# Weight gradients of a gated feed-forward block on one core: the seven block products in another order and other buffers, and the stores of transposed `dd` on another DMA queue

## The chip, the cores and the metric

The kernel runs on one core of one Trainium2 chip. The metric is the device time of one execution in microseconds; the number shown is the median of several runs. The profile is one execution taken by the hardware profiler, and its span runs from the first to the last instruction of the program. TensorE is PE in the profile (its weight loads are PEld), VectorE is DVE, ScalarE is ACT, GpSimd is POOL and SyncE is SP. SP computes nothing here: it only issues DMAs, one after the other, and an instruction of SP or POOL that waits holds up all that stand behind it on that engine.

## The reference

One layer of a transformer, forwards and backwards: layer norm, linear attention with 32 heads, a residual, layer norm again, a gated feed-forward block, a residual; the output and six gradients are returned (for the input and five weight matrices). There are 2048 rows, a width of 640 and a feed-forward width of 1728, all in bf16.

```python
def _B_ref(x, w_gate, w_up, w_down):
    g = _silu(x @ w_gate)
    u = x @ w_up
    return (g * u) @ w_down
...
x = A_x
h = x + _A_ref(_layernorm(x, axis=-1), A_wqkv, A_wo)
h2 = h + _B_ref(_layernorm(h, axis=-1), B_w_gate, B_w_up, B_w_down)
...
_out, _vjp = jax.vjp(_f, A_x, A_wqkv, A_wo, B_w_gate, B_w_up, B_w_down)
_grads = _vjp(grad_out)
```

The change lies in the feed-forward block. With `hn` the normalised rows and `dh2` the incoming gradient, `dg` and `du` are the gradients of `x @ w_gate` and `x @ w_up`, and the weight gradients are `hnᵀ dg`, `hnᵀ du` and, for `w_down`, `mᵀ dh2` with `m = g * u`.

## The kernel before

**Stages.** The program first does the attention forwards, then the second layer norm (to about 150 us of the span), then the feed-forward block forwards and backwards (about 150 to 480 us), then the gradient through both layer norms and the attention, and last the output `h2`. Only the feed-forward stage is changed.

**Groups.** That stage (L616 to L826) runs over four groups of columns of the feed-forward width, `GW = [448, 448, 448, 384]`; the text calls them group 0 to 3 and writes `w` for the width. Each group has two parts.

- *The loop* (L636 to L679) goes over the 16 row tiles of 128 rows, two at a time. PE makes `pg` and `pu` (L640, L645; in group 2 also `pdm`, L655). ACT takes them from PSUM with two sigmoids and two copies (L661 to L667). DVE makes `m`, `dg` and `du` in seven operations (L673). `m` goes to the strip `m_s`, `dg` and `du` side by side to the strips `dd[0]` (row tiles 0 to 7) and `dd[1]` (row tiles 8 to 15). For each row tile SP issues a DMA transpose `stg<-dd` (L676) into one of three staging buffers `stg`, and POOL stores that buffer to `scr_dT` in DRAM (L677), from where the next stage reads it as `cols`. For every four row tiles POOL stores `m_s` to `scr_m` (L679).
- *The dw part* (L703 to L826) makes the weight gradients on PE. `dw` (L703) makes whole products over all 16 row tiles: 16 matmuls for each part it is given. The calls are named here by what they make: `dw(0,1)`, `dw(2,3)` and `dw(4)` for the row blocks of `dh2ᵀ m`, and `dw(dgu 4)` for the last row block of `hnᵀ dg` and `hnᵀ du`. The remaining four row blocks of those two are made as one 2 by 2 block matrix product with seven products of sums in place of eight; each product is done for two row blocks `u` of 128 and has 8 matmuls for each. The sums of `hn` blocks are `S`; the sums of `dd` blocks T1, T2 and T3 are written over `B11` and `B12`, which lie in `dd[0]`, and T4 over the first half of `m_s`.

**Order.** In this stage SP, PE, DVE and ACT run in the order in which the code is written (`manual_schedule`, L616); POOL's order is chosen by the scheduler. After `dw(0,1)` and `dw(dgu 4)` PE does the seven products in the order of L783 to L824: `B11` into `pa` for both `u`, `B21` into `pd` for `u` = 0, `dw(4)`, T1 into `pc`, `B21` for `u` = 1, T1 for `u` = 1, `dw(2,3)`, and then S2 T2, S3 T3, `hn` T4 into `pa` and S4 `B22` into `pc` for the two `u` in turns. Here `pa` holds both `u` in the two halves of one PSUM tile, and each product adds to the last: after each one ACT copies the running sum out (`keep`, L772), and the differences of sums give the four results.

**Buffers.** PSUM has four tiles `mm` of two banks each; `pa`, `pd` and `pc` take three. The copies `part` that `keep` makes and the results `dwev` that go out to DRAM share six buffers (`fpool`, tag `f`) with `nsg`, `u` and `a` of the loop. A `dwev` buffer is free again when POOL's store of it (L716, L758) has landed. Four strips (tag `S`) hold `m_s`, the two `dd` and one more; a strip is taken by a tile of the next group once its last reader is done.

**After the four groups** the first PE work is `ps_dhn` (L108), 54 matmuls for a row tile, with `cols` loaded by ACT's and POOL's queues. POOL's loads `pkr` (L937) for a much later stage use the three `stg` buffers too.

## Time and profile before

| what | value |
|---|---|
| median of 3 runs | 839.43 us (837.1 to 844.32) |
| the profiled execution | 838.23 us, span 836.5 us |
| PE | 801.9 us busy, 5357 matmuls |
| DVE | 535.1 us busy |
| ACT | 286.8 us busy |
| POOL | 207.0 us busy |
| mean DMA rate | 191 GB/s |
| stores `scr_dT<-stg` | 64, of 224.0 KB (48) and 192.0 KB (16), on POOL's queue |

The parts of the profile that the prediction uses: the waits (who waited for whom, with the total, the count and the longest), the timeline (start, duration, engine, line, operation, count, and in brackets the idle time before with what ended it), groups of instructions by shape, the windows (busy time of each engine in a stretch, then the granted TensorE clock, the share of the DMA engines' time that was used, and GB/s), and for one line the time from a DMA's issue to its landing. A timeline row with x8 is eight matmuls back to back; its duration counts to the modelled end of the last one.

### The profile page before, as it was taken

How to read it: one execution, taken by the hardware profiler on the slowest of the kernel's cores; microseconds unless marked ns; L12 is line 12 of the kernel's file. 1: busy time of each engine (PE TensorE's matmuls, PEld its weight loads, DVE VectorE, ACT ScalarE, POOL GpSimd, SP SyncE). 2: the span in 40 equal slices, each digit the busy share in tenths (PEclk: the TensorE clock that was granted, in tenths of full speed). 3: DMA queues.
4: the chain of work that ended last, by engine and by line, in shares of the span. 5: the costliest groups of instructions: out<-in, count | busy, mean ns of one | idle time of the engine just before them, and what ended most of it. 6: DMA issues, size and time to landing. Idle time of an engine off the chain costs nothing.

```text
span 836.5 us, 13751 instructions
## 1 busy us (share of the span) xinstructions
PE 801.9 (96%) x5357; PEld 512.1 (61%) x5357; DVE 535.1 (64%) x955; ACT 286.8 (34%) x414; POOL 207.0 (25%) x369
## 2 busy tenths in 40 slices
PE   9999999999599979998999799999999999999998
PEld 7776566444255435544565477777777777777676
DVE  7989988784279437855593327999888456631222
ACT  6953522840175015610650122323222233332010
POOL 4600067223212321221224401211130112112230
PEclk9999999999799999999999899999999999999999
DMA  9899899898449985895388268779489959899993
GB/s 248 177 250 283 192 258 267 195 224 215 118 103 220 229 203 105 204 243 115 76 209 227 92 246 171 205 204 237 100 239 169 169 127 164 170 213 251 196 236 104
DMA packets 281585, 160.12 MB, mean 191 GB/s; under 512 B 241564, under 2 KB 267293, under 8 KB 281520
## 3 DMA queue, kind: packets, MB, share of 16 engines
q1 hardware_dynamic: 259696, 85.40, 53.8%
q0 software_dynamic: 18928, 68.52, 26.4%
q10 hardware_dynamic: 2896, 5.33, 2.0%
q8 instruction: 42, 0.69, 0.4%
q14 instruction: 23, 0.19, 0.1%
HBM read 47.68 MB, written 53.66 MB: 121 GB/s over the span
## 4 chain that ended last, share of the span: by engine, by line
PE 81%; DMA 7%; DVE 7%; issue 2%; POOL 2%; ACT 1%; ACTq 0%; POOLq 0%; DVEq 0%; SPq 0%
PE ps_dhn L108 14%; PE ps_dxn L1067 8%; PE ps_o L1125 7%; PE ps_dw L712 6%; PE ps_wa L749 5%; PE ps_dwqk L990 5%; PE ps_dm L417 5%; PE pg L640 4%; PE pu L645 4%; PE ps_kq L305 3%; DMA stg<-dd 3%; PE ps_a L571 3%; PE ps_dk L108 3%; PE ps_dp L108 3%; PE ps_gt L865 3%; PE ps_y L508 3%
## 5 line engine op out<-in xcount | busy, mean ns | idle before, releaser
L108 PE MATMUL ps_dhn<-wgT,cols 128*128 128x320 bf16 x864 | 120.7, 300 | 0.0
L108 PEld LDWEIGHTS <-cols 128*128 128x128 bf16 x864 | 84.7, 98 | 33.5 <-issue 0.3
L677 POOL DMA_DIRECT2D scr_dT<-stg x64 | 34.7, 542 | 165.9 <-DMA stg<-dd 161.1
L640 PE MATMUL pg<-wgu,hnT 128*128 128x448 bf16 (+1 forms) x320 | 63.6, 346 | 1.8 <-ACT m_s L666 1.8
L645 PE MATMUL pu<-wgu,hnT 128*128 128x448 bf16 (+1 forms) x320 | 63.6, 346 | 0.0
L712 PE MATMUL ps_dw<-m_s,dh 128*128 128x448 bf16 (+1 forms) x320 | 60.7, 346 | 1.1 <-DVE m_s L673 1.0
L1125 PE MATMUL ps_o<-wd,mT 128*128 128x320 bf16 (+3 forms) x462 | 61.1, 295 | 0.0
L146 DVE CUSTOM_DVE_ANT_0 lb_a<-lb_dy,hn 128x640 bf16<-128x640 bf16 x32 | 26.4, 825 | 54.2 <-ACT lb_dy L144 54.2
L1067 PEld LDWEIGHTS <-ring 128*128 128x128 bf16 x480 | 47.0, 98 | 18.2
L749 PEld LDWEIGHTS <-S 128*128 128x128 bf16 x256 | 25.6, 102 | 49.7 <-DVE S L736 21.1
L1125 PEld LDWEIGHTS <-mT 128*128 128x128 bf16 (+1 forms) x462 | 41.8, 97 | 17.5 <-issue 2.6
L749 PE MATMUL ps_wa<-dd,S 128*128 128x448 bf16 (+1 forms) x128 | 29.8, 382 | 23.1 <-ACT part L774 16.4
L774 ACT COPY part<-ps_wa 128x448 f32<-128x448 f32 (+1 forms) x24 | 12.4, 519 | 115.1 <-PE ps_wa L749 70.0
L1067 PE MATMUL ps_dxn<-wqkvT,ring 128*128 128x320 bf16 x320 | 51.3, 299 | 0.0
L640 PEld LDWEIGHTS <-hnT 128*128 128x128 bf16 x320 | 31.3, 98 | 29.0 <-issue 2.0
L712 PEld LDWEIGHTS <-dh 128*128 128x128 bf16 x320 | 31.3, 98 | 28.5 <-issue 1.6
L645 PEld LDWEIGHTS <-hnT 128*128 128x128 bf16 x320 | 31.3, 98 | 27.1
L417 PE MATMUL ps_dm<-wdT,dh2T 128*128 128x448 bf16 (+1 forms) x240 | 46.5, 344 | 0.0
L417 PEld LDWEIGHTS <-dh2T 128*128 128x128 bf16 x320 | 31.0, 98 | 25.1
L1132 DVE TENSOR_TENSOR h1r<-ps_o,h1r 128x640 bf16<-128x640 f32 x15 | 12.1, 823 | 52.6 <-PE ps_o L1125 45.4
L305 PE MATMUL ps_kq<-wqk,xnT 128*128 128x320 bf16 x320 | 45.1, 300 | 0.2 <-DMA xnT<-xn 0.2
L144 ACT ACTIVATE lb_dy<-ps_dhn,rstd 128x640 bf16<-128x640 f32 x16 | 12.7, 792 | 86.8 <-PE ps_dhn L108 86.8
(185 smaller groups left out, 1503.2 us busy)
## 6 DMA issues: line engine op xcount, KB each, us to landing
scr_dT<-stg POOLq DMA_DIRECT2D x48, 224.0 KB, 3.1
cols<-scr_dT POOLq DMA_DIRECT2D x6, 1728.0 KB, 8.7
scr_m<-m_s POOLq DMA_DIRECT2D x12, 448.0 KB, 4.9
cols<-scr_dT ACTq DMA_DIRECT2D x2, 1728.0 KB, 8.4
out_dram<-dwev POOLq DMA_DIRECT2D x30, 112.0 KB, 2.2
scr_dT<-stg POOLq DMA_DIRECT2D x16, 192.0 KB, 2.9
scr_pq<-pqa SPq DMA_DIRECT2D x4, 640.0 KB, 4.7
scr_xnT<-xnT SPq DMA_DIRECT2D x4, 640.0 KB, 5.1
```

Of the source, the lines that this page charges most:

```text
L108: nc.tensor.matmul(ps[:, ci, :320], lhsT=lhs(k), rhs=rhs(k, *NCH[ci]), start=(start and k == 0), stop=(stop and k == n - 1))
L146: nc.vector.tensor_tensor_reduce(out=a[:], in0=dy[:], in1=xhat, scale=1.0, scalar=0.0, op0=ALU.mult, op1=ALU.add, accum_out=sums[:, 1:2])
L305: nc.tensor.matmul(ps[:, ci, :320], lhsT=xnT[:, t, k, :], rhs=wqk[:, k, w0 + n0:w0 + n1], start=(k == 0), stop=(k == DT - 1))
L417: nc.tensor.matmul(ps[:, c, :w], lhsT=dh2T[:, kt, (t + c) * P:(t + c + 1) * P], rhs=wdT[:, kt, o:o + w], start=(kt == 0), stop=(kt == DT - 1))
L640: nc.tensor.matmul(pg[:, c, :w], lhsT=hnT[:, kt, (t + c) * P:(t + c + 1) * P], rhs=wg[:, kt, 0:w], start=(kt == 0), stop=(kt == DT - 1))
L645: nc.tensor.matmul(pu[:, c, :w], lhsT=hnT[:, kt, (t + c) * P:(t + c + 1) * P], rhs=wg[:, kt, w:2 * w], start=(kt == 0), stop=(kt == DT - 1))
L677: nc.gpsimd.dma_start(out=scr_dT[t + c, :, KO[g]:KO[g] + GK[g], :], in_=stg[:, :GK[g], :])
L712: nc.tensor.matmul(ps[:, c, :w], lhsT=lhs(t), rhs=rhs(t), start=(t == 0), stop=(t == ST - 1))
L749: nc.tensor.matmul(ps[:, u, :w], lhsT=lhs[:, t, :], rhs=rhs[:, t, :], start=(start and t == 0), stop=(t == 7), skip_group_check=not start)
L990: nc.tensor.matmul(ps[:, ci, :320], lhsT=xn_r[:, t, i * P:(i + 1) * P], rhs=dq[t // 8][:, t % 8, n0:n1] if which == 0 else dk[:, t, n0:n1] ...
L1067: nc.tensor.matmul(ps[:, ci, :320], lhsT=lhs[:, i, :], rhs=rhs[:, i, n0:n1], start=(k == 0 and i == 0), stop=(k == 2 and i == DT - 1))
L1125: nc.tensor.matmul(po(t, ci), lhsT=mTs[t // 4][r, t % 4, j, :], rhs=wd[r, j, n0:n1], start=(t, ci) not in opened, stop=last)
```

## The change

The text of the change has three parts; the matmuls and what they compute stay the same.

1. **The seven products.** `pa` becomes two PSUM tiles, `pa[0]` and `pa[1]`, one for each `u`. The products of `B11` go to the first half of these tiles and those of `B21` to the second half, all four before anything is read; `pd` is gone. Every later product is done for `u` = 0 and `u` = 1 one after the other, with ACT's copy of one between. `dw(2,3)` and `dw(4)` now stand together after the T1 products. With `pa[0]`, `pa[1]` and `pc` held, the fourth PSUM tile serves both, so the first matmul of `dw(4)` waits for DVE's copy of `dw(2,3)`. `S` has two buffers, one for each `u`, and is changed in place; `S3` has two of its own.
2. **The partial sums.** `u2` and `u3`, which were `part` buffers of `fpool`, are written as fp32 over `m_s[:, 8:16]`, the second half of the strip, once the last product that reads it is done. Only the first partial sum `s1` is still in `fpool`. The sums with `u3` and `u2` (results 1,1 and 1,0) are now one DVE operation for both `u`.
3. **The stores of transposed `dd`.** `scr_dT<-stg` is issued by SP (L719 of the changed kernel), each one after the transpose of the following row tile; the last of a group after the loop.

Also, in the loop only SP keeps the written order; PE, DVE and ACT are there ordered by the scheduler. On PE and ACT that gives the written order again; on DVE `a` moves by one place in some row tiles.

```diff
-    with tc.manual_schedule(engines={EngineType.SP, EngineType.PE, EngineType.DVE, EngineType.Activation}):
+    with tc.manual_schedule(engines={EngineType.SP}):
...
+            T1, T2, T3, T4 = B11, B11, B12, m_s[:, 0:8, :w]
+            kept = m_s[:, 8:16, :].rearrange("p t n -> p (t n)").bitcast(FP32).rearrange("p (k u n) -> p k u n", k=2, u=2)
+            u2, u3 = kept[:, 0, :, :w], kept[:, 1, :, :w]
...
+            U = range(2)
+            S = [sums.tile([P, 8, P], BF16, name="S", tag="S", bufs=2) for _ in U]
+            S3 = [sums.tile([P, 8, P], BF16, name="S3", tag="S3", bufs=2) for _ in U]
+            dw([dwd_part(0), dwd_part(1)], nc.vector.tensor_copy, first=True)
+            for u in U:
+                tt(S[u][:], hn_blk(1, 0, u), hn_blk(1, 1, u), ALU.add)
+            for u in U:
+                tt(S3[u][:], hn_blk(0, 0, u), hn_blk(1, 0, u))
+            dw([dgu_part(4, 0), dgu_part(4, 1)], copy)
+            pa = [mm("ps_wa") for _ in U]
+            pc = mm("ps_wc")
+            for u in U:
+                prod(pa[u][:, 0, :w], hn_blk(0, 0, u), B11, True)
+            for u in U:
+                prod(pa[u][:, 1, :w], hn_blk(0, 1, u), B21, True)
+            tt(T1, B12, B11)
+            ev = fw("dwev")
+            for u in U:
+                s1 = fw("s1").rearrange("p c n -> p (c n)").bitcast(FP32)[:, :w]
+                copy(out=s1, in_=pa[u][:, 0, :w])
+                tt(ev[:, u, :w], pa[u][:, 1, :w], s1, ALU.add)
+            store(ev, 0, 0)
+            for u in U:
+                prod(pc[:, u, :w], S[u], T1, True)
+                tt(S[u][:], S[u][:], hn_blk(0, 0, u))
+            tt(T2, B22, T1)
+            tt(T3, B22, B12)
+            dw([dwd_part(2), dwd_part(3)], nc.vector.tensor_copy)
+            dw([dwd_part(4)], nc.vector.tensor_copy)
+            for u in U:
+                prod(pa[u][:, 0, :w], S[u], T2, False)
+                copy(out=u2[:, u, :], in_=pa[u][:, 0, :w])
+            tt(T4, B21, T2)
+            for u in U:
+                prod(pa[u][:, 0, :w], S3[u], T3, False)
+                copy(out=u3[:, u, :], in_=pa[u][:, 0, :w])
+                tt(S[u][:], hn_blk(0, 1, u), S[u][:])
+            ev = fw("dwev")
+            tt(ev[:, :, :w], pc[:, :, :w], u3, ALU.add)
+            store(ev, 1, 1)
...
+            for u in U:
+                prod(pa[u][:, 0, :w], hn_blk(1, 1, u), T4, False)
+                copy(out=ev[:, u, :w], in_=pa[u][:, 0, :w])
+            store(ev, 0, 1)
+            for u in U:
+                prod(pc[:, u, :w], S[u], B22, False)
...
+            tt(ev[:, :, :w], pc[:, :, :w], u2, ALU.add)
+            store(ev, 1, 0)
...
+        def store_dT(g):
+            t, stg = staged.pop(0)
+            nc.sync.dma_start(out=scr_dT[t, :, KO[g]:KO[g] + GK[g], :], in_=stg[:, :GK[g], :])
...
-                    nc.gpsimd.dma_start(out=scr_dT[t + c, :, KO[g]:KO[g] + GK[g], :], in_=stg[:, :GK[g], :])
+                    staged.append((t + c, stg))
+                    if len(staged) > 1:
+                        store_dT(g)
...
+            store_dT(g)
```

POOL's order at the end of group 0, before (L677 is `scr_dT<-stg`, L679 `scr_m<-m_s`, L716 and L758 are stores of results):

```order
L679 DMA scr_m<-m_s 128x4x448
L677 DMA scr_dT<-stg 128x896 x2
L716 DMA scr_dwdT<-dwev 128x448
L677 DMA scr_dT<-stg 128x896
L716 DMA scr_dwdT<-dwev 128x448
L716 DMA out_dram<-dwev 128x448 x2
L758 DMA out_dram<-dwev 128x448
```

and in the changed kernel (L771 is `scr_m<-m_s`, L809 and L652 are stores of results):

```order
L771 DMA scr_m<-m_s 128x4x448 x4
L809 DMA scr_dwdT<-dwev 128x448 x2
L809 DMA out_dram<-dwev 128x448 x2
L652 DMA out_dram<-dwev 128x448 x2
L809 DMA scr_dwdT<-dwev 128x448 x3
```

No store of transposed `dd` stands ahead of the stores of results any more.

DVE's order in the dw part of group 0, before, from T1 (`dd<-dd`) on (L736 are all the sums, L714 is the copy in `dw`; the tiles `S` with numbers are the sums S1 to S4 for one `u`):

```order
L736 TENSOR_TENSOR dd<-dd 128x8x448
L736 TENSOR_TENSOR dwev<-ps_wd,part 128x448
L714 CAST dwev<-ps_dw 128x448
L736 TENSOR_TENSOR S_2385<-hn 128x1024
L736 TENSOR_TENSOR dwev<-ps_wd,part 128x448
L736 TENSOR_TENSOR dd<-dd 128x8x448 x2
L714 CAST dwev<-ps_dw 128x896
L736 TENSOR_TENSOR m_s<-dd 128x3584
L736 TENSOR_TENSOR S_2455<-S_2385,hn 128x1024
L736 TENSOR_TENSOR S_2477<-hn 128x1024
L736 TENSOR_TENSOR dwev<-ps_wc,part 128x448 x2
L736 TENSOR_TENSOR S_2513<-hn,S_2455 128x1024
```

and in the changed kernel (L642 are all the sums, L807 is the copy in `dw`):

```order
L642 TENSOR_TENSOR dd<-dd 128x8x448
L642 TENSOR_TENSOR dwev<-ps_wa,s_2361 128x448
L642 TENSOR_TENSOR dwev<-ps_wa,s_2364 128x448
L642 TENSOR_TENSOR S<-S,hn 128x1024 x2
L642 TENSOR_TENSOR dd<-dd 128x8x448 x2
L807 CAST dwev<-ps_dw 128x896
L807 CAST dwev<-ps_dw 128x448
L642 TENSOR_TENSOR m_s<-dd 128x3584
L642 TENSOR_TENSOR S<-hn,S 128x1024 x2
L642 TENSOR_TENSOR dwev<-ps_wc,m_s 128x896 x2
```

The sums `S` that were made behind T4 (`m_s<-dd`), between the products that read them, are now made ahead of it or before this piece; the copy of `dw(4)` has moved behind that of `dw(2,3)`, and both stand behind T2 and T3 (`dd<-dd` x2).

POOL's order at the end of group 3, before (L937 loads `pkr`, L163 fills up `scr_m` and `scr_dwdT`):

```order
L677 DMA scr_dT<-stg 128x768
L163 DMA scr_dwdT<-zpad 128x4x64
L163 DMA scr_dwdT<-zpad 128x64
L716 DMA scr_dwdT<-dwev 128x384 x2
L937 DMA pkr<-scr_pk 128x640 x3
L716 DMA out_dram<-dwev 128x384 x2
```

and in the changed kernel (L932 loads `pkr`):

```order
L163 DMA scr_m<-m_s 128x4x64 x4
L163 DMA scr_dwdT<-zpad 128x4x64
L163 DMA scr_dwdT<-zpad 128x64
L809 DMA scr_dwdT<-dwev 128x384 x2
L932 DMA pkr<-scr_pk 128x640 x3
L809 DMA out_dram<-dwev 128x384 x2
```

The three loads of `pkr` stand as before ahead of the stores of `dw(dgu 4)`, but the stores that free their `stg` buffers have gone from POOL's queue to SP's.

More of the change, by code (lines that the diff above doesn't have):

```diff
@@ L747, in prod @@
-            def prod(ps, u, lhs, rhs, start, stop):
-                for t in range(8):
-                    nc.tensor.matmul(ps[:, u, :w], lhsT=lhs[:, t, :], rhs=rhs[:, t, :],
-                                     start=(start and t == 0), stop=(t == 7), skip_group_check=not start)
-            def part32():
-                return fw("part").rearrange("p c n -> p (c n)").bitcast(FP32)[:, :w]
-            def out_w(n, m, ev, u0, nu):
-                for u in range(u0, u0 + nu):
-                    i = 2 * m + u
-                    nc.gpsimd.dma_start(out=(out_4, out_5)[n][i * P:(i + 1) * P, GO[g]:GO[g] + w], in_=ev[:, u, :w])
@@ L776 @@
-            dw([dwd_part(0), dwd_part(1)], V.tensor_copy, first=True)
-            hn_sum(1, 0)
-            dw([dgu_part(4, 0), dgu_part(4, 1)], A.copy)
-            hn_sum(2, 0)
-            hn_sum(3, 0)
-            hn_sum(4, 0)
-            pa, pd, pc = mm("ps_wa"), mm("ps_wd"), mm("ps_wc")
-            for u in range(2):
-                prod(pa, u, hn_blk(0, 0, u), B11, True, False)
-                keep(s1, u, pa)
-            sub(B11, B12, B11)
-            prod(pd, 0, hn_blk(0, 1, 0), B21, True, True)
```

89 lines of the change are left out of this document (24 added, 65 removed).

## The prediction

> **What bounds the kernel now.** I read the waits of PE first, then its timeline, then the queues behind the waits.
>
> ```profile
> PE 801.9 (96%) x5357; PEld 512.1 (61%) x5357; DVE 535.1 (64%) x955; ACT 286.8 (34%) x414; POOL 207.0 (25%) x369
> PE ps_wa L749 <- ACT part L774: 20.6, 12, 9.0
> PE ps_wa L749 <- DVE S L736: 6.8, 5, 2.2
> ```
>
> The first line is the page's: PE is busy 802 of 836.5 us, so only its idle time can be won. The other two are the two largest waits of PE in the whole program, and both stand at the block products of the feed-forward stage (L749). The windows of groups 0 to 3 of that stage and of all after it:
>
> ```profile
> 140.00:235.00 95.00, 80.44 (x415) 40.76 (x414) 54.15 (x89) 33.00 (x43) 28.19 (x50) 0.95 0.78 189
> 235.00:312.00 77.00, 72.15 (x379) 36.71 (x378) 49.84 (x77) 31.22 (x41) 19.39 (x35) 1.00 0.88 198
> 312.00:405.00 93.00, 88.15 (x464) 45.07 (x463) 58.22 (x77) 31.82 (x41) 19.45 (x35) 1.00 0.67 158
> 405.00:482.00 77.00, 70.94 (x426) 42.17 (x424) 44.09 (x77) 27.88 (x41) 27.36 (x47) 0.96 0.61 162
> 482.00:836.00 354.00, 351.69 (x2678) 253.38 (x2676) 206.42 (x424) 89.13 (x144) 64.62 (x114) 1.00 0.85 188
> ```
>
> The columns are the length, then busy time of PE, PEld, DVE, ACT and POOL, the granted clock, the share of DMA time and GB/s. The last stage has 2 us of idle PE; all that can be won lies in the first four rows. In groups 0 and 3 the clock is also below 1.00. Group 0 on PE's timeline, and ACT and POOL beside it:
>
> ```profile
> 174.33 2.43 PE L712 MATMUL ps_dw<-m_s,dh 128*128 128x448 bf16 x12
> 177.74 4.25 PE L712 MATMUL ps_dw<-m_s,dh 128*128 128x448 bf16 x20 [0.97 <-DVE m_s L673]
> 217.52 3.15 PE L749 MATMUL ps_wa<-dd,S 128*128 128x448 bf16 x8 [9.03 <-ACT part L774]
> 232.30 2.06 PE L640 MATMUL pg<-wgu,hnT 128*128 128x448 bf16 x10
> 216.94 0.53 ACT L774 COPY part<-ps_wa 128x448 f32<-128x448 f32 x1 [24.48 <-DMA out_dram<-dwev]
> 213.63 0.54 POOL L677 DMA_DIRECT2D scr_dT<-stg  x1 [4.78 <-DMA stg<-dd]
> 214.16 1.07 POOL L716 DMA_DIRECT2D out_dram<-dwev  x2
> ```
>
> From below: POOL waits for the landing of the last transpose, stores it at 213.63, and only then issues the stores of results behind it. When these land, ACT gets a buffer for its copy (216.94), and PE, which may not add to `pa` before that copy, goes on at 217.52, at first at half speed (3.15 for eight matmuls that take 1.69 in group 1, below). So a chain of transposes holds the results' stores, these the six buffers, and these PE. In group 1 there is no such long wait:
>
> ```profile
> 262.57 6.22 PE L712 MATMUL ps_dw<-m_s,dh 128*128 128x448 bf16 x32
> 268.62 6.22 PE L712 MATMUL ps_dw<-dd,hn 128*128 128x448 bf16 x32
> 297.50 1.69 PE L749 MATMUL ps_wa<-dd,S 128*128 128x448 bf16 x8 [2.21 <-DVE S L736]
> 310.62 1.68 PE L640 MATMUL pg<-wgu,hnT 128*128 128x448 bf16 x8
> ...
> PE ps_wa L749 <- DVE S L736: 3.0, 2, 2.2
> PE ps_wa L749 <- ACT part L774: 1.9, 3, 0.6
> ```
>
> The last two lines are PE's waits in the window of group 1 (total, count, longest); those of group 2 read the same. Five short ones: a product on one half of `pa` waits for ACT's copy of the other half (0.6 each), or for a sum `S` that DVE makes late (2.2 and 0.8).
>
> **The change part by part.** One matmul of width 448 costs (268.62 − 262.57) / 32 = 0.189 us. The dw part has 112 of whole products and 14 × 8 = 112 of block products, so 224 × 0.189 = 42.4 us without a wait. Group 1 takes 310.62 − 262.57 = 48.05, a loss of 5.7 (the five waits, and what it takes PE to get going after each); group 2 has the same waits; group 0 takes 232.30 − 174.33 = 57.97, a loss of 15.6.
>
> *The products in turns.* With `pa[0]` and `pa[1]`, ACT's copy of one (0.53 in the row above) and its way there and back (0.6 in all, the wait above) lie under the 1.51 us of 8 matmuls on the other. So the three 0.6 of a group go. DVE's work at each point, and T1 of group 0:
>
> ```profile
> L736 DVE TENSOR_TENSOR dd<-dd 128x3584 bf16<-128x3584 bf16 x3 | 6.0, 2020 | 6.2 <-PE ps_wa L749 6.2
> L736 DVE TENSOR_TENSOR S<-hn 128x1024 bf16<-128x1024 bf16 x4 | 2.7, 687 | 5.0 <-PE ps_wa L749 4.1 <-PE ps_wc L749 0.9
> L714 DVE CAST dwev<-ps_dw 128x896 bf16<-128x896 f32 x2 | 2.2, 1092 | 4.1 <-PE ps_dw L712 4.1
> 191.89 2.03 DVE L736 TENSOR_TENSOR dd<-dd 128x3584 bf16<-128x3584 bf16 x1 [6.14 <-PE ps_wa L749]
> ```
>
> Counted from the first block product: T1 can start at 3.0, when `B11` is no longer read, and takes 2.0, while PE does `B21` until 6.1; no wait. PE does T1 products until 9.1 and `dw(2,3)` until 15.1. DVE in that time has two adds (0.6 each), two sums (0.7 each), T2 and T3 (2.0 each), from 9.1 to about 13.9. So it is free when `dw(2,3)` ends, and the new wait of `dw(4)` is the copy alone: 1.09 and the way there and back, 1.3 us. Were DVE still busy with T3, it would be up to 2.0 more. T4 (2.0) lies under `dw(4)` and the S2 products. Behind it the sums for S4 and the first joint add (some 1.1, it waits for the last `u3`, at 26.0 of that count) end at 27.1, while PE needs them at 28.4. So the 2.2 and the 0.8 go as well. Group 1 and 2 each win 5.7 − 1.3 = 4.4 us. The waiting `dw(4)` holds all products behind it, so its 1.3 is paid in full, four times.
>
> A rule speaks against such a wait. The Trainium skill, TensorE: Matmul & The Clock Gate, in the section on a second HAM failure mode (psum-queue depth-cycling), says that short idle times of PE between groups of matmuls that cycle through PSUM can bring the clock down and up again. Here group 1, with five waits of up to 2.21, has the clock at 1.00, and only the 9.03 was followed by half speed: by the rows a short wait costs its own length. By the Trainium skill's rule it would cost more (a rival below).
>
> *The partial sums over `m_s`.* `u2` and `u3` need no `fpool` buffer, but they wait for the stores `scr_m<-m_s`. POOL now issues these with nothing of the transposes ahead. Cost nothing; cover: 15 us from the loop's end to the first `u2`.
>
> *The stores on SP's queue.* They free POOL's queue: results are stored when they are made, so the 9.03 us and the half speed behind it (3.15 − 1.68 = 1.5, and about 0.4 in the next eight matmuls) go. In group 0 there remain 1.0 at the start (DVE, `m_s`), about 0.5 more there since DVE now does `a` ahead of the last `m`, 0.4 of small gaps and the 1.3 of `dw(4)`: of the 15.6 lost, 3.2 stay, and 12.4 are won. Queued behind a waiting store on SP are the next transpose and, at a group's end, the weights' loads for the next group. Their pace rests on these rows: the page's median time from issue to landing, the transposes of group 1 (issue on SP, first and last start), the same for a stretch with a mixed queue, and one of the loads:
>
> ```profile
> scr_dT<-stg POOLq DMA_DIRECT2D x48, 224.0 KB, 3.1
> ...
> out_dram<-dwev POOLq DMA_DIRECT2D x30, 112.0 KB, 2.2
> ...
> wgu<-in_B_w_up_dram SPq DMA_DIRECT2D x3, 560.0 KB, 6.9
> ...
> stg<-dd SPq DMA_TRANSPOSE x64, 3.8
> L676 SPq DMA_TRANSPOSE stg<-dd x16: 1220/1272/1943, 241.1 to 279.7; - x16
> 293.95 0.52 SPq L190 DMA_DIRECT2D wgu<-in_B_w_up_dram  x1
> L383 SPq DMA_TRANSPOSE xnT<-xn x6: 1200/1232/2270, 30.2 to 43.1; - x6
> DMA to landing us min/median/max: 2.6/3.1/3.4
> L326 SPq DMA_DIRECT2D scr_xnT<-xnT x2: 533/552/572, 36.8 to 39.5; - x2
> DMA to landing us min/median/max: 3.6/3.7/3.7
> ```
>
> Before, a transpose waits until the store three back has landed: (3.8 + 3.1) / 3 = 2.3, and something for POOL's own queue; measured (279.7 − 241.1) / 15 = 2.6 us for a row tile. In the change the same three buffers give 2.3, the lag of one transpose gives (3.8 + 0.55) / 2 = 2.2, and SP's own issuing 1.27 + 0.55 = 1.8. The last four lines are the nearest thing that the trace has to the new queue: from 30 to 43 us SP issues transposes and stores of 640 KB in turns, and the transposes land in 3.1, the stores in 3.7. I take 2.3 to 2.6, no slower than before; the upper end, where only one landing of the pair is in flight for each of two buffers, is (3.8 + 3.1) / 2 = 3.45. What is due: `wgu` for group 2 was issued at 293.95, lands 6.9 later, 68.6 after the group's start at 232.3, and is now due at 310.6 − 232.3 − 4.4 = 73.9. SP loses some 3 by waiting for the last transpose (3.8 less the 1.27 of issuing, and 0.55 for the store). That leaves 2 us at the old pace. T1 of group 0 writes over what transposes 0 to 7 read; the row of T1 above shows that it waited for PE, not for them, so they had landed by 191.9. The bound there is two row tiles, 5 us; I take 0.
>
> *Group 3.*
>
> ```profile
> 404.08 1.79 PE L640 MATMUL pg<-wgu,hnT 128*128 128x384 bf16 x10
> 465.64 2.72 PE L749 MATMUL ps_wa<-dd,S 128*128 128x384 bf16 x8 [5.47 <-ACT part L774]
> 479.64 5.60 PE L108 MATMUL ps_dhn<-wgT,cols 128*128 128x320 bf16 x40
> 457.76 0.56 POOL L677 DMA_DIRECT2D scr_dT<-stg  x1 [0.46 <-issue]
> 460.67 1.60 POOL L937 DMA_DIRECT2D pkr<-scr_pk  x3
> ```
>
> It takes 479.64 − 404.08 = 75.6, in which 28 matmuls of `ps_dhn` are done early (28 × 5.60 / 40 = 3.9). At width 384 a matmul costs 0.189 × 384 / 448 = 0.162, so the loop's 160 and the dw part's 224 take 62.2, with 1.3 for `dw(4)` 63.5. So 75.6 − 3.9 − 63.5 = 8.2 us are won. One new wait is to be watched: POOL's `pkr` loads now wait for SP's last store; behind them stand the stores of `dw(dgu 4)`, whose buffer the first joint add takes, and on that add the last products wait. The last store was issued at 457.76, landing some 2 later (2.2 for a store of results), 55.7 after the group's start. From there a `pkr` and two stores (0.54 each), their landing (2.2) and the add (1.0) make 4.8, so 60.5 against the products at 63.5 less their own 2.6, 60.9. It fits by half a microsecond; each microsecond of delay beyond it costs one. I take 0.
>
> *Sum.* 12.4 + 4.4 + 4.4 + 8.2 = 29.4 us, against the profiled execution's 838.2 (span 836.5): 808.8. The runs shown have a median 1.2 above that execution, so the forecast is 810.
>
> **The rivals.**
>
> *The short waits stay, or one long one does* (T1 behind late transposes in group 0). For it: PE still waits for ACT's copies at every product, and margins of some 2 us depend on DMA that is busy for 0.78 and 0.88 of its time. Against it: the copies are a third of the 1.51 that covers them. Without the 4.4 of groups 1 and 2 and some 3 in group 0: 810 + 12 = 822.
>
> *The chain of transposes takes over at its upper end.* At 3.45 a row tile, 0.85 more than before, 15 row tiles cost 13 us: `wgu` lands at 68.6 + 3 + 13 = 84.6 against 73.9, so 11 late, and in group 3 POOL's stores are 12 late. 810 + 22 = 832, just under 1% faster. For it: stores and transposes now share one queue in order. Against it: the rows at 30 to 43 us.
>
> *The same, beyond it: slower than before.* If a store on SP's queue must land before the next transpose moves at all, a row tile costs 3.1 + 1.27 = 4.4, 0.95 more; 15 row tiles in each of groups 1 and 3 make 28: 860. It decides from a pace of 3.7 on, where the gain is eaten up.
>
> *The clock drops at the new waits.* Each of the four would bring eight matmuls at half speed, 4 × 1.5 = 6 us: 816. For it: half speed did follow one wait. Against it: the clock of 1.00 in groups 1 and 2 with their waits. The page of the Trainium skill named above, TensorE: Matmul & The Clock Gate, would expect it.
>
> **How the numbers follow.** Forecast 810, chance 0.64, by itself 804 to 815 (below: the 1.3 of `dw(4)` hidden too; above: 2.0 of T3 in three groups, or the margins missed by a few). Clock 816: 0.04. Waits that stay, 822: 0.16. Level, 832: 0.09. Slower, 860: 0.07. The range 803 to 824 leaves out the last two and little else. A difference of 1% is about what a measurement of this kernel can tell from none. Faster by over 1%: 0.64 + 0.04 + 0.16 and 0.02 of the 832 case, 0.86 in all; slower 0.07; the rest of that case, 0.07, the same.
>
> **What would show it.** Right: no wait over 2 us at the block products; one wait of about 1.2 for each group at `dw(4)`, put down to DVE's copy; dw parts of 44 us in groups 1 and 2 and about 45 in group 0; clock 1.00 in all four windows; stores `scr_dT` that land in 2 to 4 us on SP's queue with 2.3 to 2.6 us for a row tile. Wrong: PE waiting at `pg` of group 2 (late `wgu`), at the T1 products (late transposes), or at the last `pc` products of group 3 (`pkr`); a pace above 3.4; or waits at `dd` and `m_s` of a new group's first row tiles, where ACT and DVE wait for strips that the old group's transposes still read.

## The result and the profile after

The changed kernel takes 813.15 us (median of 4 runs, 812.56 to 815.54), the kernel before beside it 838.26 (4 runs, 834.42 to 844.32). The ratio is 0.970, 95% interval 0.964 to 0.976: 25 us or 3% faster, where 810 was forecast. The profiled execution took 812.93 us with a span of 811.2. First the page's line of PE, and the three largest waits of PE in the whole program (total, count, longest):

```profile
PE 797.0 (98%) x5357; PEld 512.0 (63%) x5357; DVE 535.7 (66%) x947; ACT 287.2 (35%) x414; POOL 173.1 (21%) x305
...
PE ps_dw L805 <- DVE dwev L807: 4.6, 4, 1.2
PE ps_wc L646 <- DVE dwev L642: 2.2, 1, 2.2
PE ps_dw L805 <- DVE m_s L763: 1.4, 2, 0.8
```

The waits of 9.03 and 5.47 us for ACT's copies are gone, and so are all the short ones at the products. In their place stand the four waits of `dw(4)`, and one of 2.2 us at the last products. The windows of groups 0 to 3 and of the rest (columns as before: PE, PEld, DVE, ACT, POOL, clock, DMA share, GB/s):

```profile
140.00:219.00 79.00, 75.40 (x401) 39.01 (x399) 53.18 (x86) 32.53 (x42) 18.94 (x32) 1.00 0.96 230
219.00:293.00 74.00, 72.82 (x386) 37.57 (x384) 49.94 (x75) 31.84 (x41) 11.14 (x19) 1.00 0.84 194
293.00:382.00 89.00, 87.82 (x466) 45.33 (x464) 58.60 (x75) 31.84 (x41) 11.15 (x19) 1.00 0.70 177
382.00:450.00 68.00, 64.77 (x389) 38.40 (x388) 44.45 (x75) 27.89 (x41) 16.96 (x28) 0.98 0.80 191
```

Groups 1 and 2 have 1.2 us of idle PE each, group 3 has 3.2 and a clock of 0.98. PE's timeline gives the dw parts of groups 0, 1 and 3, of which these are the rows that matter:

```profile
174.02 2.43 PE L805 MATMUL ps_dw<-m_s,dh 128*128 128x448 bf16 x12
...
219.43 2.06 PE L730 MATMUL pg<-wgu,hnT 128*128 128x448 bf16 x10
...
249.70 6.22 PE L805 MATMUL ps_dw<-m_s,dh 128*128 128x448 bf16 x32
...
278.29 3.19 PE L805 MATMUL ps_dw<-m_s,dh 128*128 128x448 bf16 x16 [1.18 <-DVE dwev L807]
...
293.42 2.05 PE L730 MATMUL pg<-wgu,hnT 128*128 128x448 bf16 x10
...
408.53 5.36 PE L805 MATMUL ps_dw<-m_s,dh 128*128 128x384 bf16 x32
...
440.94 2.76 PE L646 MATMUL ps_wa<-m_s,hn 128*128 128x384 bf16 x16
445.88 4.18 PE L646 MATMUL ps_wc<-dd,S 128*128 128x384 bf16 x16 [2.18 <-DVE dwev L642]
449.85 20.43 PE L108 MATMUL ps_dhn<-wgT,cols 128*128 128x320 bf16 x147
```

Group 0's dw part takes 219.43 − 174.02 = 45.4 us, where it took 57.97 before, group 1's 293.42 − 249.70 = 43.7 in place of 48.05. In group 3, 16 matmuls that take 2.76 us (row above it) take 4.18 behind the wait of 2.18. POOL and DVE in group 3 show what that wait is:

```profile
437.55 0.54 POOL L932 DMA_DIRECT2D pkr<-scr_pk  x1 [18.17 <-DMA scr_dT<-stg]
...
441.53 0.54 POOL L932 DMA_DIRECT2D pkr<-scr_pk  x1 [1.66 <-DMA scr_dT<-stg]
442.06 1.09 POOL L809 DMA_DIRECT2D out_dram<-dwev  x2
```

```profile
444.87 0.96 DVE L642 TENSOR_TENSOR dwev<-ps_wc,m_s 128x768 bf16<-128x768 f32 x1 [5.50 <-DMA out_dram<-dwev]
```

Read from below: DVE's joint add waits 5.50 us until a store of results has landed; that store is issued at 442.06, right behind the third load of `pkr`, and POOL had stood at these loads for 18.17 us until stores `scr_dT` of SP landed. It is the chain that the prediction named and priced at nothing. SP's stores were late themselves: those issued at 420.87 and 424.51 landed only after 10.5 and 7.7 us (the next ones after 2.2), while ACT's load of `cols`, issued at 420.91, was in flight. No run moves that load alone, so how much of the delay it makes stays open.

SP's transposes (L766) and stores (L719) of group 1, with the time from issue to landing:

```profile
L766 SPq DMA_TRANSPOSE stg<-dd x16: 1220/1274/1934, 228.1 to 266.0; - x16
...
DMA to landing us min/median/max: 2.9/3.7/5.6
```

```profile
L719 SPq DMA_DIRECT2D scr_dT<-stg x16: 320/568/1557, 231.1 to 269.5; - x16
DMA to landing us min/median/max: 2.0/2.5/5.6
```

The pace is (266.0 − 228.1) / 15 = 2.5 us for a row tile, 2.6 before.

### The profile page after: what moved, and what is told of

It is laid out like the page before. It is cut to its first block, busy times and chain, and to the rows that moved or that the text cites. A ratio compares the mean times of both kernels' runs of the same rounds, so it can differ in the third digit from the quotient of the medians.

```text
span 811.2 us, 13620 instructions
## 1 busy us (share of the span) xinstructions
PE 797.0 (98%) x5357; PEld 512.0 (63%) x5357; DVE 535.7 (66%) x947; ACT 287.2 (35%) x414; POOL 173.1 (21%) x305
## 4 chain that ended last, share of the span: by engine, by line
PE 85%; DVE 9%; DMA 4%; issue 1%; POOL 1%; SPq 0%; ACT 0%; ACTq 0%; DVEq 0%; POOLq 0%
PE ps_dhn L108 14%; PE ps_dxn L1062 8%; PE ps_o L1120 7%; PE ps_dw L805 7%; PE ps_wa L646 6%; PE ps_dwqk L985 5%; PE ps_dm L417 5%; PE pg L730 4%; PE pu L735 4%; PE ps_kq L305 4%; PE ps_wc L646 3%; PE ps_a L571 3%; PE ps_y L508 3%; PE ps_gt L860 3%; PE ps_dp L108 3%; PE ps_dk L108 3%
## 5 line engine op out<-in xcount | busy, mean ns | idle before, releaser
L751 ACT ACTIVATE dd<-pg 128x896 bf16<-128x896 f32 (+1 forms) x32 | 29.1, 910 | 37.3 <-PE pg L730 37.3
L305 PEld LDWEIGHTS <-xnT 128*128 128x128 bf16 x320 | 31.1, 98 | 13.1 <-DMA xnT<-xn 1.0
L985 PEld LDWEIGHTS <-hn 128*128 128x128 bf16 x320 | 31.1, 98 | 11.9
```

Of the source, the lines that this page charges most:

```text
L305: nc.tensor.matmul(ps[:, ci, :320], lhsT=xnT[:, t, k, :], rhs=wqk[:, k, w0 + n0:w0 + n1], start=(k == 0), stop=(k == DT - 1))
L751: sig = nc.scalar.activation(out=dg, in_=pg[:, :, :w], func=ACT.Sigmoid)
L985: nc.tensor.matmul(ps[:, ci, :320], lhsT=xn_r[:, t, i * P:(i + 1) * P], rhs=dq[t // 8][:, t % 8, n0:n1] if which == 0 else dk[:, t, n0:n1] ...
```

## The experiments

Twelve runs. Their times, each with its ratio to the kernel before on the same chip (before: 836.9 to 838.3; the changed kernel itself took 813.2 and 811.7 in two sets of runs, so a difference of 1.5 us between two rows says nothing by itself):

| run | edit | us, median (range) | ratio, 95% interval |
|---|---|---|---|
| r_after | the changed kernel again | 811.7 (810.3 to 813.3) | 0.969, 0.967 to 0.972 |
| e1_pkr | `pkr` off POOL's queue | 810.3 (809.8 to 814.1) | 0.969, 0.966 to 0.971 |
| e2_dw4 | `dw(4)` ahead of T1, its copy too | 818.8 (817.4 to 819.7) | 0.977, 0.975 to 0.980 |
| e3_both | e1 and e2 | 818.3 (816.9 to 822.4) | 0.978, 0.975 to 0.981 |
| e4_dw4 | `dw(4)` ahead of T1, its copy behind | 807.9 (806.4 to 809.3) | 0.965, 0.963 to 0.967 |
| e5_both | e1 and e4 | 804.9 (804.3 to 805.5) | 0.962, 0.960 to 0.964 |
| e6_pool | e5, stores `scr_dT` on POOL | 810.9 (807.7 to 813.1) | 0.969, 0.966 to 0.972 |
| p1_sp | before + stores on SP | 830.1 (829.2 to 831.6) | 0.992, 0.990 to 0.994 |
| p4_turns | products in turns alone | 824.9 (822.9 to 828.6) | 0.987, 0.982 to 0.992 |
| p3_part | turns + stores on SP | 819.3 (816.0 to 820.7) | 0.979, 0.975 to 0.983 |
| p2_prod | turns + sums over `m_s` | 812.4 (809.4 to 818.4) | 0.971, 0.968 to 0.974 |
| s1_lag0 | changed, store right behind its transpose | 845.0 (842.0 to 846.4) | 1.009, 1.006 to 1.012 |

**The changed kernel again.** No edit.

> The changed kernel again, unaltered, beside the other three on the same chip, so that differences of 4 us can be read: 812 to 815, with the wait of 2.2 us at the last pc products of group 3 and waits of 1.0 to 1.2 us at dw(4) in each group. Rival (the 2.2 us wait and the half speed behind it were chance of one execution): the time is the same but that wait is missing or below 1 us in this profile.

It took 811.7. Its waits differ from those of the first profile. PE at T1 of group 0 and at the last `pc` products of group 3, and DVE's T1:

```profile
195.38 3.19 PE L646 MATMUL ps_wc<-dd,S 128*128 128x448 bf16 x16 [2.13 <-DVE dd L642]
...
446.28 2.76 PE L646 MATMUL ps_wc<-dd,S 128*128 128x384 bf16 x16 [1.08 <-DVE dwev L642]
```

```profile
193.30 2.02 DVE L642 TENSOR_TENSOR dd<-dd 128x3584 bf16<-128x3584 bf16 x1 [8.62 <-PE ps_wa L646]
```

T1 started at 193.30, though the `B11` products, the only ones of the named group that it needs, were over near 190.1. The eighth transpose of the group, the last that reads `dd[0]`, landed at 193.23; in the first profile it landed at 190.68 and T1 did not wait. So both margins that the prediction took as zero, late transposes in group 0 and `pkr` in group 3, are paid by 0 to 2 us from one execution to the next.

**`pkr` off POOL's queue.**

```diff
-            nc.gpsimd.dma_start(out=pkrs[t][:], in_=scr_pk_v[:, t, :])
+            (nc.sync if t < 3 else nc.gpsimd).dma_start(out=pkrs[t][:], in_=scr_pk_v[:, t, :])
```

> The changed kernel with the first three loads of pkr issued on SyncE's queue, two of them around the last store of group 3 and the third much later, so that POOL holds nothing of them. Theory (in group 3 POOL is held by the pkr loads, which wait for the last stores of transposed dd; behind them stand the stores of dw(dgu 4), then the first joint add, then PE's last products): the wait of 2.2 us at the last pc products and the half speed behind it (about 1.4 us) go, clock 1.00 to the end of group 3, 3.5 us less than the changed kernel: 809 to 810. Rival A (the stores of dw(dgu 4) are late because transposes and stores share the DMA engines with the load of cols, whatever POOL does): the wait stays, 813. Rival B (the half speed at the end of group 3 has another cause than the wait): 2 us less, 811, with a granted clock still below 1.00 at the end of group 3.

POOL's store of `dw(dgu 4)` and the end of PE's group 3 in this run:

```profile
424.93 1.07 POOL L809 DMA_DIRECT2D out_dram<-dwev  x2 [4.73 <-ACT dwev L807]
```

```profile
444.38 2.76 PE L646 MATMUL ps_wc<-dd,S 128*128 128x384 bf16 x16
446.98 23.25 PE L108 MATMUL ps_dhn<-wgT,cols 128*128 128x320 bf16 x170
```

The store goes out as soon as ACT has made the result, 17 us earlier, there is no wait at the last products, and the clock is 1.00 throughout. The dw part of group 3 takes 37.6 us, where it took 449.85 − 408.53 = 41.3 in the first profile and 38.8 in the second. So the chain is shown, rival A falls, and rival B for this execution, and its price is 1.2 to 3.7 us. By the medians it is 1.4 on this chip, which the intervals don't separate from nothing.

**`dw(4)` ahead of T1, first try.** The call goes from behind `dw(2,3)` to ahead of T1.

```diff
+            dw([dwd_part(4)], nc.vector.tensor_copy)
             tt(T1, B12, B11)
...
             dw([dwd_part(2), dwd_part(3)], nc.vector.tensor_copy)
-            dw([dwd_part(4)], nc.vector.tensor_copy)
```

> The changed kernel with dw(4) moved ahead of the T1 products, so that it no longer stands right behind dw(2,3) on the PSUM tile that both use. Theory (in each group the first matmul of dw(4) waits 1.05 to 1.18 us for DVE's copy of dw(2,3), paid in full): these four waits go, 4.6 us less, 808 to 809. Rival (the wait only covers another one, for T2, T4 or a sum that DVE makes, and moves there): within 1.5 us of the changed kernel, 812 to 815, with new waits at the block products put down to DVE.

The expectation failed: 818.8, 7 us more than the changed kernel. DVE and PE in group 1:

```profile
272.94 0.62 DVE L807 CAST dwev<-ps_dw 128x448 bf16<-128x448 f32 x1 [11.64 <-PE ps_dw L805]
273.48 2.02 DVE L642 TENSOR_TENSOR dd<-dd 128x3584 bf16<-128x3584 bf16 x1
```

```profile
275.55 3.20 PE L646 MATMUL ps_wc<-dd,S 128*128 128x448 bf16 x16 [2.65 <-DVE dd L642]
```

The rival came about, but through the edit itself: `dw` also writes DVE's copy at that place, so DVE stood at the copy of `dw(4)` for 11.64 us, and T1 came behind it at 273.48, though the `B11` products were over near 266.7. The wait of 1.18 was exchanged for one of 2.3 to 2.7, four times.

**Both edits, first try.**

> Both edits at once: pkr's first loads on SyncE's queue, dw(4) ahead of the T1 products. If both theories hold the two savings are at different places and add up: 3.5 + 4.6 = 8 us less than the changed kernel, 805, and no wait of PE above 1 us is left in the four groups. Rival (the savings meet the same next bound, so that only one is paid): 808 to 810.

It took 818.3, and the waits at T1 are the same (10.3 us in all, longest 2.7). It tells nothing of whether the savings add up.

**`dw(4)` ahead of T1, its copy behind T1.** The call now stands behind the adds and the store of result 0,0; on PE the order is that of the run before.

```diff
             store(ev, 0, 0)
+            dw([dwd_part(4)], nc.vector.tensor_copy)
...
-            dw([dwd_part(4)], nc.vector.tensor_copy)
```

> The changed kernel with dw(4) ahead of the T1 products on PE as in the run before, but with DVE's copy of it written behind T1 and the two adds of result 0,0, so that DVE is free for T1 as soon as the B11 products are done. Theory (the 2.3 to 2.7 us that PE waited for T1 in the run before were DVE standing at the copy of dw(4) ahead of T1, by the order that I wrote, and not a need of T1): no wait at T1 and none at dw(4) in any group, 4.6 us less than the changed kernel, 806 to 809. Rival (T1 is late for another reason, the transposes of the first eight row tiles that still read B11): the wait at T1 stays in groups 0 to 2, 813 or more.

It took 807.9, as expected, and neither of the two waits is left in any group. The dw parts of groups 1 and 2 take 42.4 us in place of 43.7, which is the prediction's 42.4 for 224 matmuls without a wait. In group 3 a wait of 2.3 us at the last products, and half speed behind it, remain.

**Both edits.**

> That edit and the first pkr loads on SyncE's queue together. Theory: the two savings lie at different places and add up; 4.6 and 1 to 3.5 us (the wait at the last pc products was 1.1 to 2.2 in the two profiles of the changed kernel) less than the changed kernel, 804 to 807. Rival (once dw(4) is gone, PE reaches the last pc products 1 us earlier in group 3, and another chain, the stores of results that DMA lands late, takes the place of pkr's): no better than the run with dw(4) alone.

It took 804.9: 6.8 us less than the changed kernel and the fastest of all, almost 4% below the kernel before. PE in its group 0 goes over both places without a gap:

```profile
193.35 3.19 PE L805 MATMUL ps_dw<-m_s,dh 128*128 128x448 bf16 x16
196.38 3.19 PE L646 MATMUL ps_wc<-dd,S 128*128 128x448 bf16 x16
```

By the medians the two savings add up: 3.8 by `dw(4)`, and 3.0 more by `pkr` (1.4 alone). The intervals of neighbouring steps overlap a little; only the 6.8 us of both together are clear of the noise.

**The stores on SP alone.** The kernel before, with this one edit:

```diff
-                    nc.gpsimd.dma_start(out=scr_dT[t + c, :, KO[g]:KO[g] + GK[g], :], in_=stg[:, :GK[g], :])
+                    staged.append((t + c, stg))
+                    if len(staged) > 1:
+                        store_dT(g)
...
+            store_dT(g)
```

> The kernel before with one part of the change alone: the stores of transposed dd on SyncE's queue, each after the next transpose. Products, partial sums and order as before. Theory of the prediction (the chain from POOL's queue over the stores of results and the six buffers to ACT's copy makes the 9.03 us wait in group 0 and the 5.47 in group 3, the products' own order the five short waits): the two long waits and the half speed behind them go, the short waits of 5.7 us a group stay in all groups: 14 to 16 us less than before, 821 to 826 against 837 to 839. Rival (the long waits are made by too few buffers, whatever queue the stores of transposed dd are on): less than 5 us gained, the 9.03 still there.

It took 830.1, half of the gain that I expected. Group 0 did as expected: its dw part takes 49.5 us in place of 57.97, only the short waits left. Group 3 did not: 48.4 in place of 49.6. (Group 2 lost 1.3; why, is told in the last section.) The first of group 3's two long waits on PE, and POOL and ACT:

```profile
438.11 2.72 PE L758 MATMUL ps_wa<-dd,hn 128*128 128x384 bf16 x8 [3.45 <-ACT part L783]
```

```profile
451.69 0.54 POOL L946 DMA_DIRECT2D pkr<-scr_pk  x1 [18.70 <-DMA scr_dT<-stg]
...
456.18 1.08 POOL L725 DMA_DIRECT2D out_dram<-dwev  x2
```

```profile
436.44 0.40 ACTq L157 DMA_DIRECT2D cols<-scr_dT  x1
436.88 0.80 ACT L723 CAST dwev<-ps_dw 128x768 bf16<-128x768 f32 x1 [12.60 <-issue]
...
459.04 0.48 ACT L783 COPY part<-ps_wa 128x384 f32<-128x384 f32 x1 [17.64 <-DMA out_dram<-dwev]
```

The two waits have different causes. The second, 2.35 us before the product at 459.57, is the expected chain with another instruction in it: POOL now stands at `pkr` in place of the stores `scr_dT`, the results behind go out at 456.18, and ACT's partial sum, which needs their buffer, waits 17.64 us for them. The first, 3.45, is new and comes long before that. ACT stands for 12.6 us at its load of `cols`, which reads `scr_dT`; the copy of `dw(dgu 4)` and the first partial sum come behind it, and for this sum PE waits. In all nine profiles with the stores on SP behind the next transpose that load goes out 35.1 to 40.0 us after the group's start (here 436.44 − 396.80 = 39.6), in the other five 30.3 to 31.0. So in group 3 the stores' move exchanged one instruction that holds POOL for another, and lengthened another wait, ACT's at that load.

**The products and the partial sums, without the stores on SP.** In the changed kernel the three lines and the last `store_dT(g)` above become POOL's store again.

> The changed kernel with the stores of transposed dd back on POOL's queue, each issued behind its transpose: products in turns and partial sums over m_s alone. Theory, worked out again for the new use of buffers (the result of dw(0,1) is stored late in group 0, so the copy of dw(4) and the first joint add wait for a buffer; u2 and u3 need none): in group 0 only 2 to 4 us of the long wait come back, in group 3 about none; 813 to 820. Rival (the stores on SyncE's queue are what removes the long waits of groups 0 and 3, as the prediction's parts have it): 12 to 16 us lost against the changed kernel, 825 to 829, with a wait of over 5 us in group 0.

It took 812.4, just below the range expected and the same as the whole change; the rival's 825 to 829 falls. The profiled execution was the slowest of the six (818.4), so it shows the mechanism at its dearest. POOL, DVE and PE at the end of group 0:

```profile
214.95 0.54 POOL L767 DMA_DIRECT2D scr_dT<-stg  x1 [7.18 <-DMA stg<-dd]
215.48 1.07 POOL L806 DMA_DIRECT2D out_dram<-dwev  x2
```

```profile
218.82 1.09 DVE L642 TENSOR_TENSOR dwev<-ps_wc,m_s 128x896 bf16<-128x896 f32 x1 [4.73 <-DMA out_dram<-dwev]
```

```profile
219.97 4.87 PE L646 MATMUL ps_wc<-dd,S 128*128 128x448 bf16 x16 [3.64 <-DVE dwev L642]
```

POOL stores the results at 215.48, no earlier than the 214.16 of the kernel before: the whole chain from the transposes is still there. But what waits at its end is now the joint add, which PE needs only for its last products, and not `u2`, which PE needs for the S3 products. The wait is 3.64 even here, in place of 9.03. Group 3, where I expected about none, has two: 1.0 for ACT's `u2` and 3.3 for T4 (the last experiment has two like them, with their causes).

**The partial sums in buffers again**, products in turns, stores on SP:

```diff
-            u2, u3 = kept[:, 0, :, :w], kept[:, 1, :, :w]
+            u2, u3 = {}, {}
...
+            def keep(d, u):
+                d[u] = fw("part").rearrange("p c n -> p (c n)").bitcast(FP32)[:, :w]
+                copy(out=d[u], in_=pa[u][:, 0, :w])
```

The two copies call `keep(u2, u)` and `keep(u3, u)`, and the joint adds are made for each `u`.

> The changed kernel with u2 and u3 back in the six buffers of fpool; products in turns and the stores on SyncE's queue stay. Theory (a partial sum that needs a buffer waits for the store of dw(dgu 4), which in group 3 stands behind pkr on POOL): groups 0 to 2 as in the changed kernel, in group 3 a wait of 6 to 9 us at the S3 products put down to ACT's copy in place of the 1.1 to 2.2 at the last pc products; 5 to 7 us more than the changed kernel, 816 to 820. Rival (the prediction's: the partial sums over m_s are worth nothing once the stores are off POOL's queue): 812 to 815.

It took 819.3. PE's longest wait:

```profile
PE ps_wa L649 <- ACT part L642: 7.7, 1, 7.7
```

It stands in group 3, where `u2` now waits for the buffer whose store is behind `pkr`. The sums over `m_s`, which the prediction priced at nothing, are worth 7.6 us here (819.3 against 811.7; 0.9 to 1.0% by the ratios).

**The products in turns alone** (both last edits):

> Products in turns alone: stores of transposed dd back on POOL's queue and u2 and u3 back in fpool. Theory (the products in turns take away only the short waits; a partial sum in a buffer brings the long waits back in groups 0 and 3): a wait of 7 to 10 us in group 0 and of 5 to 8 in group 3 at the S3 products, put down to ACT's copy; 7 to 12 us more than with the sums over m_s, 819 to 825. Rival (the long waits came from the old order of the products, not from the buffers of u2 and u3): no wait above 4 us, 811 to 816.

```profile
PE ps_wa L649 <- ACT part L642: 10.7, 2, 6.0
```

It took 824.9. The long waits are back, in group 0 with 4.6 us (shorter than expected) and in group 3 with 6.0; the time is as expected. From here the sums over `m_s` save 12.6 us (p2) and the stores on SP 5.6 (p3, with intervals that just touch).

**The chain of transposes, made slower.** In the changed kernel each store is issued right behind its own transpose:

```diff
-                    if len(staged) > 1:
-                        store_dT(g)
+                    store_dT(g)
...
-            store_dT(g)
```

> The changed kernel with each store of transposed dd issued by SyncE right behind its own transpose, in place of behind the next one, so that SyncE waits for every landing. Theory (the pace of the chain is then one landing, 2.9 to 3.9 us, and 0.57 for the store, about 4.0 for a row tile, beyond the point of 3.7 that the prediction's slower rival named): the weights for group 2 come about 6 us late and the last stores of group 3 about 14; 825 to 840. Rival (SyncE's issuing overlaps enough that the lag does not matter, or the margins are wider than I worked out): within 3 us of the changed kernel.

It took 845.0, slower than the kernel before and 5 us above the range expected. SP's transposes in group 2, and PE's waits:

```profile
L766 SPq DMA_TRANSPOSE stg<-dd x16: 1222/1278/2125, 327.0 to 392.7; - x16
```

```profile
PE ps_wc L646 <- DVE dd L642: 14.5, 2, 9.1
PE pg L730 <- DMA wgu<-in_B_w_gate_dram: 11.2, 1, 11.2
```

The pace is (392.7 − 327.0) / 15 = 4.4 us a row tile. The late weights are at the place that the theory named (11 us in place of 6); at T1 of groups 0 and 3 PE waits for DVE, which waits for the transposes of `dd[0]`. The lag of one transpose is what makes SP's queue bear both.

**The best version with the stores back on POOL.** The edit of p2 on e5.

> The best version so far (dw(4) early, pkr's first loads on SyncE's queue) with the stores of transposed dd back on POOL's queue, so that the pair shows what those stores on SyncE's queue are worth when nothing else waits. Theory (results stand again behind the last stores of transposed dd; in group 0 the first joint add waits for the buffer of dw(dgu 4), in group 3 for the results' stores too): 5 to 10 us more than with the stores on SyncE's queue, 810 to 816, with a wait of 3 to 5 us at the last pc products of group 0. Rival (with the sums over m_s and the products in turns the queue of these stores is worth nothing, as the two medians 812.4 and 811.7 suggest): 804 to 807.

It took 810.9 against 804.9, with intervals that lie apart (0.966 to 0.972 and 0.960 to 0.964): the stores on SP are worth 6 us where nothing else waits. The waits are not where I put them: group 0 pays 1.1, and the longest stands in group 3, one product earlier than the last. PE, POOL and DVE there:

```profile
442.34 4.06 PE L646 MATMUL ps_wa<-m_s,hn 128*128 128x384 bf16 x16 [3.17 <-DVE m_s L642]
```

```profile
436.60 1.08 POOL L806 DMA_DIRECT2D scr_dwdT<-dwev  x2
```

```profile
439.66 0.96 DVE L804 CAST dwev<-ps_dw 128x768 bf16<-128x768 f32 x1 [8.78 <-DMA scr_dwdT<-dwev]
```

POOL stores the result of `dw(0,1)` at 436.60, behind its last store of transposed `dd` at 434.76. DVE's copy of `dw(2,3)` waits 8.78 us for such a buffer, T4 stands behind that copy, and PE waits 3.17 for T4. Ahead of the S3 products PE has also waited 1.79 for ACT's copy of `u2`, and ACT 13.75 for a store `scr_m<-m_s`, which stands among the stores `scr_dT` on POOL.

## Why the prediction was right, and where it was not

**The sum.** Forecast were gains of 12.4, 4.4, 4.4 and 8.2 us in groups 0 to 3. Measured, by the dw parts of the first profile: 57.97 − 45.41 = 12.6, 48.05 − 43.72 = 4.3, again 4.3, and in group 3, where the prediction's own 75.6 − 3.9 = 71.7 stands against 449.85 − 382.53 = 67.3, 4.4. That is 25.6 together, and the span fell by 25.3. All of the shortfall is in one term, group 3.

**Group 3.** The step that failed is "It fits by half a microsecond; each microsecond of delay beyond it costs one. I take 0." The mechanism was right, the size wrong: the last store landed 58.4 us after the group's start, where 55.7 was forecast (issued 1.8 later, 2.9 in place of 2 in flight), the third `pkr` was issued at 441.53, 0.6 behind that landing, and the joint add started at 444.87, where PE wanted its result at 443.7. It cost 2.18 us and half speed over the next 3.4 us (1.4 more). Without the loads on POOL the wait is gone (e1). A margin of half a microsecond that rests on the landing of a DMA is no margin: the same kernel paid 1.08 in its other profile.

**T1 in group 0.** "The bound there is two row tiles, 5 us; I take 0." It held in the first profile by 0.2 us (landing at 190.68, the `B11` products over near 190.9), and cost 2.1 in the second. The rival named for it has a real mechanism, at a sixth of its price (2.1 of 12).

**The wait at `dw(4)`.** Forecast 1.3, measured 1.18 (1.05 in group 3), once in each group, put down to DVE's copy. That it is paid in full is shown by e4, which gets back 1.3 in each of groups 1 and 2.

**What the parts are worth.** Here the prediction was wrong in its reasons, though not in the total; that the total came out all the same is in part luck, since both parts were in the change and it did not matter which of them earned the gain. It put the gains of groups 0 and 3 down to the stores on SP ("They free POOL's queue: results are stored when they are made, so the 9.03 us and the half speed behind it (3.15 − 1.68 = 1.5, and about 0.4 in the next eight matmuls) go") and took the sums over `m_s` for nothing ("Cost nothing"). The runs:

| | sums in buffers | sums over `m_s` |
|---|---|---|
| products in turns, stores on POOL | 824.9 | 812.4 |
| products in turns, stores on SP | 819.3 | 811.7 and 813.2 |

The old order of products has 837 to 838 with the stores on POOL and 830.1 with them on SP. The chain from the transposes to PE has a link at each end. The stores on SP cut its beginning, but in group 3 `pkr` takes their place on POOL. The sums over `m_s` cut its end, since what PE needs early no longer takes a buffer; with the stores on POOL it does not cut it clean, as `u2` then waits for `scr_m<-m_s` (1.8 us of PE in e6, 1.0 in p2). Either cut does much of the work of the other, so the parts don't add: the stores on SP are worth 7 us on the kernel before and 5.6 beside the turns. With the sums over `m_s` the medians differ by under 1, either way, but by 6 once `dw(4)` and `pkr` are out of the way (e5 against e6). Why so little shows in the first pair stays open: the profiled execution of p2 does have 6 us more in the dw parts, but it is the slowest of its six, and no profile of a usual one was taken. Sums over `m_s` with the old order of products were not tried.

**The pace and the slower rival.** 2.5 us for a row tile was measured in group 1 (forecast 2.3 to 2.6), 3.0 in groups 2 and 3, where the loop's 45 us or the load of `cols` sets it, and 3.3 in group 0 (3.5 before). That a slow enough pace turns the sign is shown: at 4.4 the time is 845 (s1), where the slower rival said 860 for the same pace. It was 15 too dear; its point of 3.7 lies between the paces measured, but no run tested it. The reason in s1 is not the rival's, though: there SP waits for each transpose to land before it issues the store, while the rival had the next transpose wait for the store. In the change as made neither arose. Nor did the level rival's pace of 3.45 come about in groups 1 and 3, on which its price rests.

**The clock.** None of the waits at `dw(4)` was followed by half speed, in 28 cases over seven profiles, so that rival fell. But "only the 9.03 was followed by half speed: by the rows a short wait costs its own length" did not hold for the wait of 2.18, and was a misreading already: in the kernel before the 5.47 of group 3 was followed by half speed too (eight matmuls took 2.72 us there, 1.46 at full speed). The sum is not touched by it, since group 3 was taken as a whole. The last section has the rule that the traces give.

## What to carry to other kernels

When a wait ends on a long chain (a queue, a buffer, a copy), price each part of a change with the others undone: two cuts of one chain are worth little more than one, and the next instruction on the queue may take the place of the one that was moved. Look at what else of the same queue waits for the thing that was moved away; here three loads for a stage almost 200 us later held the results of this one. When an order is changed on one engine, write down where the copies that go with it land on the other (e2 against e4: 11 us).

## What the runs showed of the hardware

**Half speed comes by windows, not by the length of a wait.** All changes of the granted clock within a profile lie a whole number of 3.413 us apart (in the profile of before, for one, 211.48 and 464.07 us, 74 times that). Over the 14 profiles, outside the first 20 us and the end, I cut the span at this grid and added up PE's idle time in each piece. Of the pieces at full speed, all 20 with 2.08 us or more of idle PE were followed by a piece at half speed, of five with 2.00 to 2.05 two were, and of 52 with 1.0 to 1.99 none. The windows of the changed kernel's group 3, cut at its grid, and of e2 in two groups, whose wait at T1 was 2.65 us in both (length, then PE, PEld, DVE, ACT, POOL, clock, DMA share, GB/s):

```profile
443.63:447.04 3.41, 1.23 (x9) 0.70 (x8) 0.96 (x1) 0.48 (x1) 3.10 (x7) 1.00 0.82 239
447.04:450.45 3.41, 3.41 (x13) 1.66 (x12) 0.35 (x1) 0.00 (x0) 1.32 (x4) 0.50 1.00 390
```

```profile
195.57:198.98 3.41, 1.87 (x10) 0.78 (x8) 1.50 (x2) 0.00 (x0) 0.54 (x1) 1.00 1.00 228
198.98:202.39 3.41, 2.30 (x13) 1.21 (x14) 2.69 (x4) 0.00 (x0) 1.07 (x2) 1.00 1.01 244
...
362.81:366.22 3.41, 0.76 (x5) 0.23 (x4) 2.68 (x3) 0.00 (x0) 0.54 (x1) 1.00 1.01 202
366.22:369.63 3.41, 3.41 (x10) 1.41 (x11) 1.25 (x3) 0.00 (x0) 1.07 (x2) 0.50 0.99 212
```

In the upper fence PE is busy for 1.23 of 3.41 us, and the next piece runs at 0.50. In the lower, the wait at 199 us falls on both sides of a cut and costs only its length; that at 364 lies within one piece, and the next 3.4 us run at half speed. So the same wait may or may not cost 1.4 to 1.7 us more, by where it falls; that is why the waits of 2.21 in groups 1 and 2 of the kernel before cost nothing more (cuts at 296.81 and 388.97 fall into them), and the 2.18 after did. In p1 the wait of 2.21 in group 2 lies within one piece (379.65 to 383.06); the next one runs at half speed, and that dw part takes 49.35 in place of 48.05. The Trainium skill, TensorE: Matmul & The Clock Gate, in What's actually happening, has such a window of 3413 ns that runs freely; the grid of 3.413 us above agrees with it. The same page of the Trainium skill, in Why this matters for your kernels, asks for no idle gaps above about 3 us; here 2.1 us within one window was enough, and the measurement decides.
